# Top-k attention and routed experts on one core: where the pieces of one search stand among those of the next

## The chip, the cores and the metric

The kernel runs on one core of a Trainium2 chip. The metric is the device time of one execution in microseconds (us). Three executions of the kernel before took 1707.5, 1709.06 and 1711.37 us; the median is 1709.06.

PE is the matrix engine, DVE the vector engine, ACT the scalar engine, POOL GpSimd, SP the engine whose queue issues most of the loads. Each engine takes its instructions in order and stands at the first whose input or buffer is not there.

## The reference

Attention over 8 batches, 8 heads, 576 tokens, 64 wide, in which each row keeps only its 32 largest scores; then a layer of 8 experts, one per token.

```python
def _attn_ref(q, k, v):
    scores = scale * np.matmul(q, k.transpose(0, 1, 3, 2))
    kth = np.partition(scores, -top_k, axis=-1)[..., -top_k:-top_k + 1]
    scores = np.where(scores >= kth, scores, -1000000000.0)
    attn = np.exp(scores - np.max(scores, axis=-1, keepdims=True))
    attn = attn / (np.sum(attn, axis=-1, keepdims=True) + 1e-09)
    return np.matmul(attn, v)

def _moe_ref(x, w_gate, w1, w2):        # x: 4608 tokens x 512
    logits = x @ w_gate
    expert_idx = np.argmax(logits, axis=1)
    ...
    for e in range(E):                  # tokens sorted by expert
        h = np.maximum(x_sorted[lo:hi] @ w1[e], 0.0)
        y_sorted[lo:hi] = h @ w2[e]
    return gate_w[:, None] * y_sorted[inv_perm]
```

## The kernel before

The work of attention is cut into 32 units, one for a batch and two heads. The 576 rows of a head are four tiles of 128 and a rest of 64. A unit has five searches: four over a pair of tiles (the same tile of both heads) and one over the single tile that holds both rests. So there are 160 searches, five to a unit and twenty to a batch.

One search goes through all engines. PE multiplies scores (`products`, L234). ACT copies them from PSUM (`scores`, L243, tile `s`). DVE folds each row into halves, the larger and the smaller of two elements (`fold`, L250 and L251, tile `hl`), and finds the 32nd largest in four rounds of `max` and `match_replace` (`search`, L273 to L295, result `thr`). POOL makes `low` from it (L297). ACT turns scores below the threshold into a huge penalty (`depths`, L309, tile `w`), POOL subtracts (`less`, L318) and ACT takes the exponential (`weights`, L329). PE transposes the weights (`transposed`: the four large blocks `wTm`, L342, then the rest `wTl`, L350), and ACT copies both back (L345, L347, L353, L355).

After its last search a unit has an end (`outputs`, `ending`): the products with `v` in two halves of the query columns (`po`, L372), the copy to `oT` (L375), transposes and gate logits (`px`, `pl`, copied to `lt` and `x`), the divisors on DVE (L397 to L400), the logits and the scaled rows on POOL (`logits`, L405 to L408, and `rows`, L416). The last unit of a batch also routes it (`route`): DVE takes the largest logit (`mx`, L421) and ranks the tokens, and five indirect DMAs from POOL scatter the rows into `x_rows`, sorted by expert (L466).

An expert block is 128 rows of one expert: a load of rows and weights (`load_block`, on SP's queue), 16 pieces on PE (eight of `ph`, L572, and eight of `py`, L581), the result `y` on ACT (L584) and a store by an indirect DMA from POOL (L585). Batches from the third on have blocks of rows already sorted: 4, 4, 5, 4, 5 and 4 of them are computed a few pieces at a time between the searches (`pieces`), 14 after them, the last two of the former being kept back for the routing of the last batch.

The order on PE, ACT and DVE is the order of the code in `loop` (`tc.manual_schedule`). Scores are multiplied four searches ahead and copied three ahead. In search `i` come the DVE part, `depths` and `less` of `i`, the transposes of `i - 1`, half of the expert pieces, the copies of the scores of `i + 3` between the exponentials of `i`, the products of `i + 4`, and the other half of the pieces. The steps of a unit's end are a generator that goes on at named places (`at_place`). On POOL only the instructions marked `in_turn` keep the program's order; a store is put behind the last subtraction known, and a planner places it.

Of the kernel before, what the change touches and what calls it, by code (L numbers as in the profile page):

```python
# [9 lines left out]
F32 = mybir.dt.float32  # L10
# [33 lines left out]
def kernel(  # L44
# [98 lines left out]
    def token_ids(t, b):  # L143
        nc.gpsimd.iota(t, pattern=[[P, KC]], base=b * S, channel_multiplier=1)
# [30 lines left out]
    scattered = []  # L175
# [158 lines left out]
    def transposed(n, tiles, w):  # L334
        pair = len(tiles) == 2
# [3 lines left out]
        for m, i in enumerate(tiles):  # L339
# [17 lines left out]
    def outputs(n, x):  # L357
# [3 lines left out]
        po = []  # L361
        for j in range(2):
            q = slice(j * HF, (j + 1) * HF)
            po.append(bank("po"))
            for c in range(KC):
                for h in range(2):
# [5 lines left out]
                    nc.tensor.matmul(po[j][r, 0:HF], lhsT, rhs, start=(c == 0), stop=(c == KC - 1))  # L372
# [45 lines left out]
    def route(x, lg):  # L418
# [45 lines left out]
        def scatter(i):  # L464
# [5 lines left out]
            if not k.exact:  # L470
                tc.add_manual_dep(put, k.last_pool.name, AFTER)
                for other in mine:
                    tc.declare_no_dep(put, other, reason="the rows of one batch go to different places")
                mine.append(put)
# [63 lines left out]
    def load_block(expert, piece):  # L538
# [5 lines left out]
        if not k.exact:  # L544
            for put in scattered:
                tc.add_manual_dep(got, put.name, WAIT)
        n.w1 = k.wp.tile([P, 1, DT, F], F32, name="w1")
# [13 lines left out]
    def block(n, following=lambda: None):  # L561
# [23 lines left out]
        put = nc.gpsimd.indirect_dma_start(  # L585
            out=out[:, :], out_offset=bass.IndirectOffsetOnAxis(ap=n.x[:, 0, Dm + 1:XW].bitcast(I32), axis=0),
            in_=y[:, :], in_offset=None, bounds_check=N - 1, oob_is_err=False,
        )
        if not k.exact:
            tc.add_manual_dep(put.ins, k.last_pool.name, AFTER)  # L590

    PIECES = 2 * FT
    FIRST = 10
    ARRIVED = 10
# [3 lines left out]
    with ExitStack() as st:  # L598
# [9 lines left out]
        waiting, loaded, coming, spare, scatters = [], [], [], [], []  # L608
        current = None
# [5 lines left out]

        def following():
            if loaded:
                turned(loaded[0])

        def pieces(n):  # L620
            nonlocal current, left
            while n > 0 and left > 0:
                if current is None:
# [3 lines left out]
                    current = block(now, following)  # L627
                    ahead()
                if next(current, "end") == "end":
# [15 lines left out]
        def ending(b, u):  # L645

            n = unit[b * U + u]
            if u == 0:
                x_of[b] = k.xp.tile([P, KC, XW], F32, name="x")
                token_ids(x_of[b][:, :, Dm + 1].bitcast(I32), b)  # L650
# [244 lines left out]
```

## Time and profile before

| | |
|---|---|
| median of three runs | 1709.06 us |
| profiled execution | 1716.52 us, span 1714.6 us |
| PE, DVE, ACT, POOL busy | 1429.6, 1306.2, 928.1, 672.6 us |
| weight loads on PE busy | 916.1 us |
| mean granted clock of PE | 0.887 |
| DMA, all queues | 230.65 MB, mean 135 GB/s |

The span is the time from the first to the last instruction. Busy time is a share of the whole span, in which the attention part (the first 1,420 us) and the expert part (the rest) have different limits. An instruction's idle time is that of its engine just before it; behind the arrow stands what ended it. A line such as L318 is a line of the kernel above.

### The profile page before, as it was taken

What the parts mean: (1) busy time and instruction counts of PE and PEld (TensorE: products, weight loads), DVE (VectorE), ACT (ScalarE), POOL (GpSimd) and SP (SyncE); (2) the same over time, 40 slices, a digit from 0 to 9 for tenths busy, and PEclk for the clock granted to TensorE, in tenths of its full rate; (3) what the DMA queues carried; (4) which work ended last, traced back from release to release, by engine and by line L of the source; (5) the groups of instructions that cost most, each with busy time, mean ns of one, the idle gap of its engine ahead of it and who ended that gap; (6) DMA issues with size and microseconds to landing.
All of it is one profiled execution on the core that took longest, in us unless ns stands there. A gap on an engine that the chain in (4) does not pass through costs nothing. (4 is left out here: it accounts for less than half of the span.)

```text
span 1714.6 us, 24871 instructions
## 1 busy us (share of the span) xinstructions
PE 1429.6 (83%) x7874; PEld 916.1 (53%) x7874; DVE 1306.2 (76%) x4261; ACT 928.1 (54%) x1937; POOL 672.6 (39%) x993
## 2 busy tenths in 40 slices
PE   5788777867898899879987899889888889699996
PEld 3444444434555555545555555556555556477664
DVE  7999999989998899889968999889869992000000
ACT  4666666656676576656655676556655663111111
POOL 2444454435444545444434545444434453000000
PEclk8666677666999899989998999899999999899998
DMA  1000010004333433324433334343542424788884
GB/s 57 23 22 22 28 44 22 23 28 137 138 132 139 149 138 133 139 98 165 156 132 137 135 133 143 134 148 139 186 167 69 139 108 180 273 297 310 314 297 148
DMA packets 102188, 230.65 MB, mean 135 GB/s; under 512 B 5150, under 2 KB 25630, under 8 KB 102048
## 3 DMA queue, kind: packets, MB, share of 16 engines
q1 hardware_dynamic: 95904, 210.06, 34.4%
q0 software_dynamic: 6144, 18.92, 3.0%
q8 instruction: 64, 1.05, 0.3%
q14 instruction: 76, 0.62, 0.1%
HBM read 207.68 MB, written 22.33 MB: 134 GB/s over the span
## 5 line engine op out<-in xcount | busy, mean ns | idle before, releaser
L318 POOL TENSOR_TENSOR w<-s,w 128x576 f32<-128x576 f32 x288 | 412.2, 1450 | 264.9 <-ACT w L309 264.1
L234 PE MATMUL sc<-qkb 64*128 64x288 f32 (+1 forms) x1280 | 344.4, 514 | 70.9 <-ACT s L243 61.7
L273 DVE MAX8 tops<-scr 128x8 f32<-128x288 f32 x864 | 355.4, 448 | 2.2
L581 PE MATMUL py<-w,hT 128*128 128x512 f32 x640 | 319.3, 629 | 8.9 <-ACT hT L577 8.7
L572 PE MATMUL ph<-xTs,w 128*128 128x128 f32 x2560 | 312.2, 280 | 1.4 <-DMA w<-in_moe_w_dram 0.7
L572 PEld LDWEIGHTS ph<-xTs,w 128*128 128x128 f32 x2560 | 302.5, 196 | 16.4 <-issue 15.4
L309 ACT ACTIVATE w<-s,low 128x576 f32<-128x576 f32 x288 | 209.3, 770 | 180.7 <-POOL low L297 179.7
L234 PEld LDWEIGHTS sc<-qkb 64*128 64x128 f32 (+1 forms) x1280 | 172.3, 210 | 223.5 <-ACT s L243 173.6
L282 DVE MATCH_REPLACE8 scr<-tops,scr 128x288 f32<-128x288 f32 x576 | 251.0, 443 | 0.0
L329 ACT ACTIVATE w<-w,nbias 128x576 f32<-128x576 f32 x288 | 224.4, 780 | 0.3 <-POOL w L318 0.3
L342 PEld LDWEIGHTS wTm<-ident,w 128*128 128x128 f32 x1152 | 150.5, 159 | 85.6 <-issue 67.0
L342 PE MATMUL wTm<-ident,w 128*128 128x128 f32 x1152 | 187.2, 309 | 10.5 <-ACT x L391 7.3
L345 ACT COPY wT<-wTm 128x512 f32<-128x512 f32 x256 | 139.2, 583 | 92.5 <-PE wTm L342 92.4
L243 ACT COPY s<-sc 128x576 f32<-128x576 f32 x288 | 181.4, 631 | 9.8 <-PE sc L234 9.8
L581 PEld LDWEIGHTS py<-w,hT 128*128 128x128 f32 x640 | 115.2, 197 | 126.7 <-issue 111.3
L585 POOL DMA_INDIRECT out_dram<-y,xg x40 | 46.0, 1150 | 345.5 <-ACT y L584 323.3
L372 PE MATMUL po<-wT,vb 128*64 128x288 f32 x1024 | 156.3, 453 | 24.2 <-ACT wT L347 24.2
L250 DVE TENSOR_TENSOR hl<-s 128x576 f32<-128x576 f32 (+1 forms) x160 | 134.0, 837 | 40.6 <-ACT s L243 40.6
L350 PE MATMUL wTl<-ident,w 128*64 128x128 f32 x288 | 70.7, 323 | 111.8 <-ACT wT L345 111.6
L297 POOL TENSOR_SCALAR low<-thr 128x2 f32<-128x2 f32 (+1 forms) x160 | 36.5, 228 | 254.8 <-DVE thr L295 219.4
L282 DVE MATCH_REPLACE8 scr<-tops,hl 128x288 f32<-128x288 f32 x288 | 125.4, 442 | 0.0
L372 PEld LDWEIGHTS po<-wT,vb 128*64 128x64 f32 x1024 | 74.3, 150 | 95.6 <-ACT wT L347 35.2
(123 smaller groups left out, 1359.8 us busy)
## 6 DMA issues: line engine op xcount, KB each, us to landing
w<-in_moe_w_dram SPq DMA_DIRECT2D x80, 2048.0 KB, 12.4
qkb<-in_qk_dram SPq DMA_DIRECT2D x32, 576.0 KB, 3.7
xg<-x_rows SPq DMA_DIRECT2D x40, 257.0 KB, 2.8
vb<-in_v_dram SPq DMA_DIRECT2D x32, 320.0 KB, 3.1
x_rows<-blank SPq DMA_DIRECT2D x9, 257.0 KB, 2.9
x_rows<-x,posi POOLq DMA_INDIRECT x40, 3.1
out_dram<-y,xg POOLq DMA_INDIRECT x40, 3.0
wg<-in_moe_w_gate_dram SPq DMA_DIRECT2D x1, 16.0 KB, 1.9
```

Of the source, the lines that this page charges most:

```text
L234: nc.tensor.matmul(ps[rows, j, 0:HF], n.q[d, cols], n.k[d, j * HF:(j + 1) * HF], start=True, stop=True)
L243: lambda m=m, ps=ps: nc.scalar.copy(s[:, m, :, :], ps[:, :, 0:HF]) for m, ps in enumerate(got)
L273: nc.vector.max(out=tops[:, m, r * 8:(r + 1) * 8], in_=src[m])
L282: nc.vector.match_replace(out=scr[:, m, :], in_to_replace=tops[:, m, r * 8:(r + 1) * 8], in_values=src[m], imm_value=NEG,)
L309: nc.scalar.activation(w[:, m, :], s[:, m, :, :].rearrange("p j k -> p (j k)"), AF.Relu, scale=-STEEP, bias=low[:, m:m + 1],)
L318: k.last_pool = in_turn(nc.gpsimd.tensor_tensor(w[:, m, :], s[:, m, :, :].rearrange("p j k -> p (j k)"), w[:, m, :], op=ALU.subtract)).ins
L329: nc.scalar.activation(w[:, m, :], w[:, m, :], AF.Exp, scale=scale, bias=nbias[:, m:m + 1], accum_out=n.z[:, c + m:c + m + 1],)
L342: nc.tensor.transpose(pm[:, c * P:(c + 1) * P], w[:, m, c * P:(c + 1) * P], ident)
L345: nc.scalar.copy(n.wT[:, :, m, tiles[0] * P:(tiles[0] + 1) * P], pm4)
L372: nc.tensor.matmul(po[j][r, 0:HF], lhsT, rhs, start=(c == 0), stop=(c == KC - 1))
L572: nc.tensor.matmul(ph[:, f, :], n.w1[:, 0, dt, fc * P:(fc + 1) * P], n.xT[:, dt, :], start=(dt == 0), stop=(dt == DT - 1),)
L581: nc.tensor.matmul(py, hT[:, f, :], n.w2[:, 0, f, :], start=(f == 0), stop=(f == FT - 1))
```

## The change

A unit's end now begins after its fourth pair, not after the single tile. The first half of the output products needs only the queries of the first three pairs and is issued there; each half is copied to `oT` right behind `depths`, at a new place `"relu"`. The second half follows after the single tile's transposes. The divisors come one search later and POOL's logits one search later than before, and so does the routing; `FIRST` and `ARRIVED`, the searches at which a batch's new blocks begin, go from 10 to 12.

The copies of scores stand right behind `depths` and ahead of the copies of the transposes. The expert pieces of a search are spread anew over the five searches of a unit (`share`), also over the one that had none, and their first half stands between `wTm` and `wTl`. The fold of the single tile and that of the next unit's first pair both stand in the search of the fourth pair; the single tile has a buffer of its own (`hl1`).

A block's `y` is made at the start of the next pieces or behind the next subtraction, and its store is put off to the next call of `put_stores`, behind a subtraction or in the middle of the next block. Token numbers keep the program's order on POOL. Scatters no longer wait for loads of blocks that were fetched before.

```diff
@@ fold
-        hl = k.att.tile([P, 2, 2, HF], F32, name="hl")
+        hl = k.att.tile([P, 2, 2, HF], F32, name="hl") if len(tiles) == 2 else k.att.tile([P, 2, 1, HF], F32, name="hl1", bufs=1)
@@ transposed, between the copies of wTm and the transposes wTl
+        yield
@@ outputs
         for j in range(2):
             q = slice(j * HF, (j + 1) * HF)
-            po.append(bank("po"))
+            po = bank("po")
...
             yield
-        for j in range(2):
-            nc.scalar.copy(oT[:, j * HF:(j + 1) * HF], po[j][:, 0:HF])
+            nc.scalar.copy(oT[:, q], po[:, 0:HF])
             yield
@@ block
-            yield
+            yield "last" if f == FT - 1 else None
...
+        put_off(store)
+        def put_stores():
+            nonlocal current, ended
+            while stores:
+                stores.pop(0)()
+            if ended == "last":
+                ended = next(current, "end")
+                current = None
@@ ending
+            yield "products"
             next(out_steps)
+            yield "relu"
+            next(out_steps)
+            yield "weights"
             yield "products"
             next(out_steps)
...
             yield "weights"
             next(out_steps, None)
+            yield "small"
+            divisors(n)
             yield "begun"
             logits(n, lg)
             rows(n, x)
@@ loop
                 def between():
-                    if i + 1 < len(work):
-                        hl_of[i + 1] = fold(work[i + 1][2], s_of[i + 1])
+                    if len(g) == 2:
+                        fold_to(i + 1 if i + 1 < len(work) and len(work[i + 1][2]) == 2 else i + 2)
...
                 less(g, s_of.pop(i), w_of[i])
+                put_stores()
                 scatter(1)
+                at_place("relu")
...
+                share = 0.5 if g in (groups[0], groups[-2]) else 1.6 if g == groups[2] else 1.2 if g == groups[1] else 1
+                now = max(0, min(int(credit * share + 0.5), room))
+                credit = min(credit - now, 4 * rate)
+                if i + AHEAD < len(work):
+                    s_of[i + AHEAD], steps = scores(got_of.pop(i + AHEAD))
+                    for step in steps:
+                        step()
                 at_place("turn")
                 if i:
-                    turn(i - 1)
...
-                weights(n, g, w_of[i], nbias, steps)
+                    turns = turning(i - 1)
+                    next(turns)
+                pieces(now - now // 2)
+                if i:
+                    next(turns, None)
+                weights(n, g, w_of[i], nbias)
                 if i + AHEAD + 1 < len(work):
                     multiply(i + AHEAD + 1)
+                if g == groups[-2]:
+                    end = ending(b, u)
+                    late.append([end, next(end)])
                 at_place("products")
                 at_place("weights")
-                pieces(now - now // 2)
+                pieces(now // 2)
```

On POOL, around the first store of an expert block; before, it stands behind the subtraction of the second search after a unit, and the logits (`lt`, `lg`, `x`) of that unit right behind it.

```order
L275 TENSOR_SCALAR nbias<-tops_88 128x2
L297 TENSOR_SCALAR low<-thr 128x2
L300 TENSOR_TENSOR over<-tops_88,thr 128x2
L318 TENSOR_TENSOR w<-s,w 128x576 x2
L585 DMA out_dram<-y,xg 4608x512
L275 TENSOR_SCALAR nbias<-tops_90 128x2
L405 TENSOR_TENSOR lt<-lt,rz_98 128x80
L407 TENSOR_TENSOR lg<-lg,lt 128x40
L408 TENSOR_TENSOR lg<-lg,lt 128x40
L416 TENSOR_TENSOR x<-x,rz_98 128x5x128
L297 TENSOR_SCALAR low<-thr 128x2
```

Now, at the same place:

```order
L275 TENSOR_SCALAR nbias<-tops_90 128x2
L297 TENSOR_SCALAR low<-thr 128x2
L300 TENSOR_TENSOR over<-tops_90,thr 128x2
L318 TENSOR_TENSOR w<-s,w 128x576 x2
L590 DMA out_dram<-y,xg 4608x512
L275 TENSOR_SCALAR nbias<-tops_92 128x2
L405 TENSOR_TENSOR lt<-lt,rz_98 128x80
L407 TENSOR_TENSOR lg<-lg,lt 128x40
L408 TENSOR_TENSOR lg<-lg,lt 128x40
L416 TENSOR_TENSOR x<-x,rz_98 128x5x128
L297 TENSOR_SCALAR low<-thr 128x2
```

The rows are alike, but the search they belong to is one later: `tops_92` where it was `tops_90`.

On PE, from a pair's transposes to the end of a unit, in the part where expert pieces (`ph`, `py`) run beside the searches; before:

```order
L342 MATMUL wTm<-ident,w 128x128 x8
L350 MATMUL wTl<-ident,w 64x128 x2
L581 MATMUL py<-w_5311,hT 128x512
L234 MATMUL sc<-qkb 128x288 x4
L581 MATMUL py<-w_5311,hT 128x512
L342 MATMUL wTm<-ident,w 128x128 x4
L350 MATMUL wTl<-ident,w 64x128
L372 MATMUL po<-wT,vb 64x288 x8
L372 MATMUL po<-wTt,vb 64x288 x2
L234 MATMUL sc<-qkb 64x288 x4
L372 MATMUL po<-wT,vb 64x288 x8
L372 MATMUL po<-wTt,vb 64x288 x2
```

And now:

```order
L373 MATMUL po<-wT,vb 64x288 x8
L373 MATMUL po<-wTt,vb 64x288 x2
L343 MATMUL wTm<-ident,w 128x128 x8
L575 MATMUL ph<-xTs,w_5365 128x128 x8
L352 MATMUL wTl<-ident,w 64x128 x2
L234 MATMUL sc<-qkb 128x288 x4
L560 MATMUL xtp<-ident,xg 128x128 x4
L584 MATMUL py<-w_5367,hT 128x512
L343 MATMUL wTm<-ident,w 128x128 x4
L584 MATMUL py<-w_5367,hT 128x512
L352 MATMUL wTl<-ident,w 64x128
L234 MATMUL sc<-qkb 64x288 x4
```

The first half of the output products stands ahead of the transposes of the unit's last pair, the second half follows these rows, and pieces of an expert block (two of `ph`, one of `py`) stand between `wTm` and `wTl`.

On DVE, inside the short search of the first unit's single tile, after its third `match_replace`; before:

```order
L273 MAX tops_92<-scr 128x8
L282 MATCH_REPLACE scr<-tops_92,scr 128x288
L250 TENSOR_TENSOR hl<-s 128x576
L251 TENSOR_TENSOR hl<-s 128x576
L273 MAX tops_92<-scr 128x8
```

And now, in the search of the pair before it:

```order
L282 MATCH_REPLACE scr<-tops_90,scr 128x288 x2
L250 TENSOR_TENSOR hl_1064<-s 128x288
L251 TENSOR_TENSOR hl_1064<-s 128x288
L250 TENSOR_TENSOR hl<-s 128x576
L251 TENSOR_TENSOR hl<-s 128x576
L273 MAX tops_90<-scr 128x8 x2
```

The next unit's first pair (128x576) is folded right behind the single tile (128x288).

## Rows read from the trace of the kernel before

**Rows 1.** The page: busy time of the engines, and DVE in 40 slices.

```profile
PE 1429.6 (83%) x7874; PEld 916.1 (53%) x7874; DVE 1306.2 (76%) x4261; ACT 928.1 (54%) x1937; POOL 672.6 (39%) x993
...
DVE  7999999989998899889968999889869992000000
```

**Rows 2.** Waits of DVE, 64 to 1423 us: total us, times, longest.

```profile
DVE mx L421 <- POOL lg L408: 41.1, 7, 13.4
DVE hl L250 <- ACT s L243: 34.8, 20, 4.5
```

**Rows 3.** Stretches: length, busy of PE, PEld, DVE, ACT, POOL, clock, DMA, GB/s.

```profile
64.00:438.00 374.00, 286.93 (x1276) 160.91 (x1274) 360.16 (x1169) 235.34 (x499) 172.59 (x261) 0.69 0.15 50
438.00:614.80 176.80, 151.71 (x896) 96.72 (x893) 163.76 (x535) 112.88 (x237) 82.58 (x120) 0.95 0.32 115
614.80:793.60 178.80, 153.06 (x903) 96.98 (x900) 164.62 (x534) 113.08 (x239) 84.25 (x121) 0.95 0.38 134
793.60:984.70 191.10, 164.33 (x970) 109.19 (x966) 163.47 (x535) 112.85 (x239) 82.91 (x121) 0.95 0.42 150
984.70:1164.30 179.60, 154.86 (x922) 98.16 (x919) 166.35 (x534) 115.61 (x243) 85.12 (x123) 0.95 0.37 133
1164.30:1355.60 191.30, 163.19 (x974) 108.13 (x969) 163.43 (x535) 112.81 (x240) 83.24 (x120) 0.96 0.42 150
1355.60:1422.90 67.30, 57.85 (x383) 41.68 (x379) 60.78 (x192) 44.65 (x96) 35.24 (x53) 0.95 0.39 137
1422.90:1479.90 57.00, 39.38 (x242) 27.15 (x241) 8.81 (x50) 12.54 (x29) 10.36 (x13) 0.91 0.49 169
1479.90:1714.60 234.70, 214.56 (x1192) 152.87 (x1192) 0.00 (x0) 34.72 (x57) 14.68 (x15) 0.97 0.76 277
```

**Rows 4.** Stretches of one unit, without and with expert blocks.

```profile
227.60:267.60 40.00, 30.39 (x141) 16.99 (x140) 39.16 (x124) 26.06 (x56) 20.37 (x30) 0.75 0.10 33
614.80:655.40 40.60, 37.06 (x234) 23.62 (x229) 39.32 (x125) 28.44 (x62) 19.94 (x29) 1.00 0.39 140
```

**Rows 5.** Instructions in order of time, 900 to 904 us: start, length.

```profile
901.02 1.04 POOL L585 DMA_INDIRECT out_dram<-y,xg  x1 [13.56 <-ACT y L584]
...
903.34 0.20 DVE L421 TENSOR_REDUCE mx<-lg 128x5 f32<-128x40 f32 x1 [13.44 <-POOL lg L408]
```

**Rows 6.** Waits of POOL, 64 to 1423 us.

```profile
POOL out_dram L585 <- ACT y L584: 78.2, 16, 13.6
```

**Rows 7.** Waits of PE, 64 to 1423 us.

```profile
PE wTl L350 <- ACT wT L345: 105.1, 103, 6.4
PE sc L234 <- ACT s L243: 54.2, 80, 1.2
```

**Rows 8.** Instructions in order of time, from the last threshold to the tail.

```profile
1417.84 0.16 DVE L295 TENSOR_REDUCE thr<-both 128x1 f32<-128x9 f32 x1
...
1432.11 0.60 PE L342 MATMUL wTm<-ident,w 128*128 128x128 f32 x4
...
1479.91 1.08 PE L557 MATMUL xtp<-ident,xg 128*128 128x128 f32 x4 [15.35 <-DMA xg<-x_rows]
```

**Rows 9.** The page's costliest groups: busy us, mean ns, idle before.

```profile
L243 ACT COPY s<-sc 128x576 f32<-128x576 f32 x288 | 181.4, 631 | 9.8 <-PE sc L234 9.8
...
L372 PE MATMUL po<-wT,vb 128*64 128x288 f32 x1024 | 156.3, 453 | 24.2 <-ACT wT L347 24.2
```

**Rows 10.** Instructions in order of time, 643.5 to 646 us.

```profile
643.54 1.40 POOL L318 TENSOR_TENSOR w<-s,w 128x576 f32<-128x576 f32 x1 [3.67 <-ACT w L309]
643.64 1.92 DVE L250 TENSOR_TENSOR hl<-s 128x576 f32<-128x576 f32 x1
...
645.48 0.75 DVE L251 TENSOR_TENSOR hl<-s 128x576 f32<-128x576 f32 x1
```

**Rows 11.** Groups by shape on DVE, 64 to 1423 us.

```profile
L250 DVE TENSOR_TENSOR hl<-s 128x576 f32<-128x576 f32 x121 | 105.2, 869 | 34.8 <-ACT s L243 34.8
...
L250 DVE TENSOR_TENSOR hl<-s 128x288 f32<-128x288 f32 x31 | 22.4, 723 | 0.0
```

More of the change, by code (lines that the diff above doesn't have):

```diff
@@ L143, in token_ids @@
     def token_ids(t, b):
-        nc.gpsimd.iota(t, pattern=[[P, KC]], base=b * S, channel_multiplier=1)
+        return nc.gpsimd.iota(t, pattern=[[P, KC]], base=b * S, channel_multiplier=1)
     NTOP = 4
@@ L473, in scatter @@
                     tc.declare_no_dep(put, other, reason="the rows of one batch go to different places")
+                for other in fetched:
+                    tc.declare_no_dep(put, other, reason="new rows go behind all full blocks")
                 mine.append(put)
@@ L559, in turned, with block @@
         nc.scalar.copy(n.xT, ps)
-    def block(n, following=lambda: None):
+    def block(n, following=lambda: None, put_off=lambda store: store()):
         if not hasattr(n, "xT"):
@@ L607 @@
         x_of, lg_of = {}, {}
-        waiting, loaded, coming, spare, scatters = [], [], [], [], []
-        current = None
+        waiting, loaded, coming, spare, scatters, stores = [], [], [], [], [], []
+        current = ended = None
         left = 0
@@ L620, in pieces @@
         def pieces(n):
-            nonlocal current, left
+            nonlocal current, left, ended
+            if ended == "last":
+                ended = next(current, "end")
+                current = None
             while n > 0 and left > 0:
@@ L626, in pieces @@
                         turned(now)
-                    current = block(now, following)
+                    current = block(now, following, stores.append)
                     ahead()
-                if next(current, "end") == "end":
+                ended = next(current, "end")
+                if ended == "end":
                     current = None
@@ L658, in ending @@
                 load_values(unit[b * U + u + 2])
-            yield "weights"
-            next(out_steps)
-            yield "small"
-            divisors(n)
-            yield "turn"
+            yield "relu"
             next(out_steps)
@@ L695, in ending, with turning @@
                 scatter(0)
-        late, place = None, None
+        late = []
         def at_place(name):
-            nonlocal place
-            if place == name:
-                place = next(late, None)
+            for end in list(late):
+                if end[1] == name:
+                    end[1] = next(end[0], None)
+                    if end[1] is None:
+                        late.remove(end)
         got_of, s_of, hl_of, w_of = {}, {}, {}, {}
-        def turn(i):
+        folded = set()
+        def turning(i):
             b, u, g = work[i]
-            transposed(unit[b * U + u], g, w_of.pop(i))
+            return transposed(unit[b * U + u], g, w_of.pop(i))
         def multiply(i):
@@ L714, in multiply, with fold_to @@
                 unit.append(load_unit(*units[b * U + u + 2]))
+        def fold_to(i):
+            for j in range(i + 1):
+                if j < len(work) and j not in folded:
+                    folded.add(j)
+                    hl_of[j] = fold(work[j][2], s_of[j])
         def loop():
-            nonlocal late, place, credit, rate
+            nonlocal credit, rate
             for i in range(min(AHEAD, len(work))):
@@ L723, in loop @@
             multiply(AHEAD)
-            hl_of[0] = fold(work[0][2], s_of[0])
+            fold_to(0)
             for i, (b, u, g) in enumerate(work):
@@ L782 @@
         pieces(ALWAYS * PIECES)
-        for _ in current:
-            pass
+        put_stores()
+        put_stores()
         any_p = k.small.tile([P, 1], F32, name="any_p")
@@ L832 @@
                         weights(n, g, w, nbias)
-                        transposed(n, g, w)
+                        for _ in transposed(n, g, w):
+                            pass
                     for _ in outputs(n, x):
```

51 lines of the change are left out of this document (22 added, 29 removed).

## The prediction

> **What bounds the kernel now.** I read the engine table and the slices first, then DVE's waits, then a table of stretches, and only then single places. The engine table says little by itself: PE is the busier engine over the whole, DVE the second [rows 1]. The slices split the program in two: DVE is at nine tenths or close to it from the second slice to the thirty-third and does nothing in the last six, where only expert blocks are left on PE [rows 1]. So the first 1,420 us are the top-32 search on DVE, and the last 235 us are PE alone. What the change can shorten is the first part, and the passage between the two.
>
> DVE's waits between 64 and 1,423 us have two causes: the routing of a batch waits for POOL's logits, 41.1 us in seven waits, and a fold waits for the copied scores, 34.8 us in 20 [rows 2]. I cut the span where DVE starts `doubt` (L397), which happens once per unit of work (five searches), so that a stretch is a whole number of units, and call a stretch without expert blocks bare, one with four blocks per batch light, one with five heavy [rows 3]. The bare stretch of nine units is 374.0 us with 360.2 busy on DVE. The three light stretches of four units are 176.8, 178.8 and 179.6. The two heavy ones are 191.1 and 191.3, though DVE has no more to do there (163.5 and 163.4 busy, against 163.8 to 166.4). PE does have more, 164 against 152 to 155.
>
> A unit that nothing disturbs shows what is left when the waits go: 0.84 us idle on DVE in 40.0 bare, 1.28 in 40.6 light, and there PE is idle 3.54 [rows 4]. Everything above these is what the change may win.
>
> Where the waits come from is seen at 901 us. POOL stood 13.56 us at the store of an expert block's output, since ACT had not yet made `y`; the logits were queued behind the store, and DVE stood 13.44 us for them [rows 5]. POOL waited so 78.2 us in all in this part [rows 6]. Whatever POOL holds back (`low`, the subtraction) comes late to ACT and then to PE: PE waited 105.1 us for ACT's copy before the small transposes `wTl` and 54.2 for the copied scores [rows 7].
>
> **The change part by part.**
>
> Stores in fixed places, `y` earlier, logits one search later. The store now stands behind the subtraction of a search, at least one search after the block ended, and the logits go to POOL two searches after their copy from PSUM instead of one. The store itself still costs POOL its 1.04 us [rows 5], beside idle time. What is queued behind it is `nbias` and, in one search of each unit, the logits; `low`, which ACT waits for, follows them but is due some 8 us later, a fifth of a unit of 40. This removes the POOL wait, and with it most of both DVE waits. Token numbers and the undeclared order between scatter and block loads only take away waits of POOL; I cost them at nothing.
>
> Bare stretch: 374.0 less 360.2 leaves 13.8 idle; nine units at 0.84 keep 7.6. Gain **6**.
>
> Light stretches: 535.2 in all, DVE busy 494.7, idle 40.5; twelve units at 1.28 keep 15.4. Gain **25**. Bounds: 10 if more than half of the waits come back in other shapes, 40 if the remaining idle goes too.
>
> Heavy stretches: 382.4 in all. DVE's floor is 326.9 and eight units at 1.28, so 337. PE's floor is its busy time, 327.5, and what it must idle. PE takes over here, so its idle time decides. Between nothing and the 3.54 of an undisturbed light unit I take 2 per unit, because expert pieces now stand between the large transposes `wTm` and `wTl`, so that ACT's copy has a cover of one to four pieces where it had none. That gives 343.5. Gain **39**; bounds 27 (at 3.54) and 45 (DVE's floor).
>
> Last stretch (67.3, DVE idle 6.5): the first pieces of a batch now come two searches later, so six more pieces fall into these 1.6 units. A piece is worth 0.7 of PE, from the heavy stretches' mean of 163.8 against the first two light ones' 152.4, over 16 pieces more. 4.2 more on PE's 57.9, with 2 idle per unit, makes 65. Gain **2**.
>
> Passage to the tail (57.0 us): the chain goes from the last threshold at 1417.84 through the last transposes at 1432.11 to the first tail block at 1479.91, and PE idles 15.35 at its end [rows 8], so what is cut from the chain comes off the time as far as that idle time lasts. Half of a unit's output products move ahead of the last search: 156.3 us over 32 units is 4.9, so 2.4 for a half [rows 9]. A store no longer stands before the logits, 1.0. The 14.3 us from threshold to transposes are mostly backlog: the one subtraction in them needs 1.4 [rows 10]. I take a third off, 4.6. Gain **8**, bounds 0 and 16 (nothing, or all but those 1.4).
>
> Folds. A pair's fold is 0.75 us alone and was 1.92 beside POOL's subtraction [rows 10]; the mean over 121 is 869 ns and of the half-width ones 723 [rows 11]. Over 0.75 and half of that, the first fold instruction of each search loses 121 x 0.12 + 31 x 0.35 = 25 us. The pair that was folded inside the short search of a single tile now goes one search earlier, behind that tile's own fold, so the short search meets the subtraction no more. I take half of the loss, less the heavy stretches where PE decides: gain **11**. Bounds: 25 gained, or 25 more lost, if the four folds in a row meet POOL's work of their own search.
>
> Splitting the copies of scores from the exponentials adds and removes no instruction; its cost is the order on ACT alone, and is in the PE idle time above and in a rival below. Output halves free a PSUM bank earlier; nothing waits for it in the rows, so nothing is counted.
>
> The sum is 6 + 25 + 39 + 2 + 8 + 11 = 91 us. The profiled execution took 1716.5 us (span 1714.6), so 1625.5 for it. The median of the three runs shown is 1709.1, 7.5 lower; a median is what will be compared, so I forecast **1618**.
>
> **Rivals.**
>
> PE becomes the engine for good. For it: PE is 85% busy in the light and heavy stretches, and its work is now cut into more, smaller pieces. Against it: the undisturbed light unit has 3.54 us to spare. If the heavy stretches gain nothing and the light ones half, 91 - 39 - 12 = 40: 1669.
>
> The folds collide more. POOL's logits and row scaling move to the very search that now has four folds in a row (2.25 us by 0.75 and its half). If one fold per unit is held as at 643.64 us, 1.17 us times 31 is 36, and the 11 are not gained: 1618 + 47 = 1665. Against it: the row scaling stood beside a fold before, too. The rule for this is in the Trainium skill, page "SBUF — State Buffer", section "Who interferes with whom": a VectorE instruction with two inputs in SBUF and a GpSimd one that reads SBUF exclude each other for a whole instruction, whichever came first. By that rule, the trace agrees: the subtraction had begun 0.10 us before the fold that took 1.92.
>
> Slower: the scores' copies now stand before ACT's copies of the transposes. Each search of a pair puts two of them at 631 ns [rows 9], 1.26 us, between `wTm` and `wTl`. The light, heavy and last stretches hold 21.6 units and so 86 such searches: 109 us on PE. Its idle time of 3.54 per unit takes 76; 33 are left, DVE's waits return as waits for scores, and only the bare stretch and the passage gain 14: 1709 + 33 - 14 = 1728. It decides from the point at which fewer than two pieces (1.4 us) stand between the two transposes. The new order has one to four there, and the one only beside the single tile, where PE has the output products besides. So it is unlikely.
>
> Better: the unit falls to DVE's floor everywhere, 6 + 40 + 45 + 2 + 14 + 20 = 127: 1582.
>
> **How the numbers follow.** The forecast and what lies near it, 57%; PE as the engine, 17%; better, 13%; colliding folds, 7%; slower, 4%; the waits merely change places and nothing comes of it, 2%. The forecast's own range is 1600 to 1640. With the better case partly in and the two near 1665 almost, I give 1596 to 1660. Differences of up to 0.2% cannot be told from none for this kernel. Faster 95%, same 1%, slower 4%.
>
> **What would show it.** Right: POOL's wait for `y` before the tail under 15 us; DVE's wait for logits under 8; PE's wait for the copy before `wTl` halved; the four units of a light stretch near 168 us and of a heavy one near 172; the last threshold to the first tail block under 52. Wrong: heavy stretches over 182 (PE is the engine), or the folds' mean over 0.95 us, or new waits of PE at `wTl` of over 1 us per search.

## The result, and the profile after

Four executions of the changed kernel took 1629.21 us in the median (1624.39 to 1631.53), beside 1710.21 us (1707.5 to 1712.86) for the kernel before: a ratio of 0.9523 [0.9495, 0.955], 81 us faster. The profiled execution took 1630.09 us (span 1628.1, mean granted clock 0.896), 86.4 us less than the one of before.

The page of the changed kernel, engines and DVE's slices, answers to [rows 1]:

```profile
PE 1334.4 (82%) x7874; PEld 869.4 (53%) x7874; DVE 1285.3 (79%) x4261; ACT 916.7 (56%) x1937; POOL 672.9 (41%) x993
...
DVE  7999999999999999999998999999989972000000
```

DVE has the same 4261 instructions and 20.9 us less busy time. They fill the same 34 slices, but a slice is now 40.7 us long instead of 42.9. PE has the same 7874 and 95 us less busy time, which no step of the prediction counted on.

Stretches of the changed kernel, with the columns and the rule for the cuts of [rows 3] (`doubt` now stands one search later, so the first cut is 7.3 us later too):

```profile
71.30:430.60 359.30, 237.06 (x1263) 137.38 (x1263) 347.85 (x1169) 230.62 (x499) 174.47 (x261) 0.75 0.15 49
430.60:598.70 168.10, 146.43 (x904) 96.64 (x904) 162.71 (x535) 111.70 (x238) 84.19 (x120) 0.92 0.36 128
598.70:769.80 171.10, 150.08 (x902) 96.06 (x902) 164.04 (x535) 112.11 (x238) 83.80 (x121) 0.91 0.39 140
769.80:940.70 170.90, 152.34 (x976) 101.31 (x976) 162.27 (x535) 113.01 (x241) 83.74 (x122) 0.96 0.47 168
940.70:1110.50 169.80, 148.09 (x913) 95.78 (x911) 162.89 (x535) 112.47 (x240) 82.16 (x121) 0.94 0.40 141
1110.50:1281.80 171.30, 152.89 (x975) 101.79 (x975) 162.67 (x534) 112.95 (x241) 83.81 (x122) 0.95 0.46 164
1281.80:1338.20 56.40, 50.94 (x325) 35.58 (x324) 51.95 (x167) 37.11 (x79) 30.07 (x46) 0.97 0.37 139
```

A heavy stretch now takes as long as a light one, 168 to 171 us: DVE, busy for 162 to 164 of them, sets both. DVE's waits in 71.3 to 1338.2 us, beside [rows 2]:

```profile
DVE base L445 <- ACT rk L440: 7.3, 7, 2.2
DVE hl L250 <- ACT s L243: 6.5, 2, 3.2
```

The waits for the logits are gone and those for the scores fell from 34.8 us to 6.5. The longest in total are now the routing's waits for ACT's copy of the ranks (`rk`), which were 1.1 us before. POOL's list of waits for the same stretch has no wait for `y` (78.2 before, [rows 6]). But PE waits as long as it did [rows 7]:

```profile
PE wTl L352 <- ACT wT L346: 110.3, 48, 6.1
```

It waits seldom and long instead of often and briefly, and DVE no longer has to wait with it.

### The profile page after: what moved, and what is told of

It is laid out like the page before. It is cut to its first block, busy times and chain, and to the rows that moved or that the text cites. A ratio compares the mean times of both kernels' runs of the same rounds, so it can differ in the third digit from the quotient of the medians.

```text
span 1628.1 us, 25051 instructions
## 1 busy us (share of the span) xinstructions
PE 1334.4 (82%) x7874; PEld 869.4 (53%) x7874; DVE 1285.3 (79%) x4261; ACT 916.7 (56%) x1937; POOL 672.9 (41%) x993
## 5 line engine op out<-in xcount | busy, mean ns | idle before, releaser
L318 POOL TENSOR_TENSOR w<-s,w 128x576 f32<-128x576 f32 x288 | 405.2, 1426 | 289.4 <-ACT w L309 289.4
L575 PEld LDWEIGHTS ph<-xTs,w 128*128 128x128 f32 x2560 | 300.1, 193 | 26.8 <-issue 25.1
L584 PE MATMUL py<-w,hT 128*128 128x512 f32 x640 | 308.7, 614 | 5.5 <-ACT hT L580 5.4
L234 PE MATMUL sc<-qkb 64*128 64x288 f32 (+1 forms) x1280 | 244.1, 506 | 69.4 <-ACT s L243 63.1
L343 PE MATMUL wTm<-ident,w 128*128 128x128 f32 x1152 | 179.6, 295 | 43.2 <-ACT oT L375 34.1
L234 PEld LDWEIGHTS sc<-qkb 64*128 64x128 f32 (+1 forms) x1280 | 124.0, 208 | 142.8 <-ACT s L243 80.2
L343 PEld LDWEIGHTS wTm<-ident,w 128*128 128x128 f32 x1152 | 138.7, 150 | 110.7 <-ACT oT L375 40.7
L297 POOL TENSOR_SCALAR low<-thr 128x2 f32<-128x2 f32 (+1 forms) x160 | 34.8, 217 | 353.2 <-DVE thr L295 329.2
L243 ACT COPY s<-sc 128x576 f32<-128x576 f32 x288 | 169.9, 637 | 9.6 <-PE sc L234 9.6
L373 PE MATMUL po<-wT,vb 128*64 128x288 f32 x1024 | 171.7, 488 | 0.6 <-ACT wT L348 0.6
L352 PE MATMUL wTl<-ident,w 128*64 128x128 f32 x288 | 65.3, 303 | 124.9 <-ACT wT L346 123.7
L250 DVE TENSOR_TENSOR hl<-s 128x576 f32<-128x576 f32 (+1 forms) x160 | 129.7, 811 | 12.0 <-ACT s L243 12.0
L373 PEld LDWEIGHTS po<-wT,vb 128*64 128x64 f32 x1024 | 80.9, 164 | 88.7 <-issue 34.1
```

The costliest lines, as they stand in the source:

```text
L234: nc.tensor.matmul(ps[rows, j, 0:HF], n.q[d, cols], n.k[d, j * HF:(j + 1) * HF], start=True, stop=True)
L243: lambda m=m, ps=ps: nc.scalar.copy(s[:, m, :, :], ps[:, :, 0:HF]) for m, ps in enumerate(got)
L318: k.last_pool = in_turn(nc.gpsimd.tensor_tensor(w[:, m, :], s[:, m, :, :].rearrange("p j k -> p (j k)"), w[:, m, :], op=ALU.subtract)).ins
L343: nc.tensor.transpose(pm[:, c * P:(c + 1) * P], w[:, m, c * P:(c + 1) * P], ident)
L373: nc.tensor.matmul(po[r, 0:HF], lhsT, rhs, start=(c == 0), stop=(c == KC - 1))
L575: nc.tensor.matmul(ph[:, f, :], n.w1[:, 0, dt, fc * P:(fc + 1) * P], n.xT[:, dt, :], start=(dt == 0), stop=(dt == DT - 1),)
```

## The experiments

All ratios are to the kernel before on the same chip. Losses are differences of these ratios times 1714 us, the time of before beside these runs; the changed kernel's own ratio is uncertain by 0.003, or 5 us, and so is each loss measured against it. Waits are read from 64 to 1330 us; in slower runs the attention part lasts longer, so there this window leaves out more of it.

| run | what is different from the changed kernel | median us | ratio |
|---|---|---|---|
| e1_store_at_once | `y` and store at the block's end | 1642.5 | 0.9576 [0.9563, 0.9589] |
| e4_logits_early | divisors, logits, routing a search earlier | 1633.59 | 0.9513 [0.9495, 0.9531] |
| e9_store_and_logits_back | both | 1676.87 | 0.9788 [0.9764, 0.9811] |
| e2_copies_between | score copies between the exponentials | 1791.69 | 1.0468 [1.0447, 1.0489] |
| e6_pieces_after | no pieces between `wTm` and `wTl` | 1657.99 | 0.9671 [0.9653, 0.9689] |
| e8_copies_and_pieces_back | both | 1689.58 | 0.9863 [0.9841, 0.9885] |
| e10_four_back | all four | 1743.77 | 1.0158 [1.0132, 1.0184] |
| e5_before_stores_off | the kernel before, with late stores alone | 1697.0 | 0.9908 [0.9892, 0.9925] |
| e3_folds_apart | folds where they were | 1631.4 | 0.9514 [0.9499, 0.9529] |
| f1_even_shares | pieces spread more evenly | 1624.37 | 0.9498 [0.9484, 0.9512] |
| f2_cover_fourth | f1, more pieces in one gap | 1627.32 | 0.9504 [0.9482, 0.9527] |
| f3_cover_and_early_logits | f2 with e4 | 1630.99 | 0.953 [0.9517, 0.9543] |

**The stores and the logits.** First each undone alone.

```diff
-                    current = block(now, following, stores.append)
+                    current = block(now, following)
...
-                if ended == "end":
+                if ended == "last":
+                    next(current, "end")
+                    ...
```

> The changed kernel, but y and its store are issued at once when an expert block's last piece is done, as before the change; all else stays. Theory A (the store that waits for y holds up POOL, and most of DVE's waits come from there): POOL waits 50 us or more for y again before the tail, DVE waits 30 to 60 us more, about 1665 us. Theory B (the waits went because the logits have one search more, and the copies of the scores stand earlier): POOL waits for y, but DVE does not feel it, 1630 to 1638 us.

It lost 9 us. POOL waits for `y` again, but DVE's waits hardly change: it stands 11.3 us for scores and not at all for logits. The loss is in DVE's busy time. From the first `doubt` to the last this run takes 18 us longer (the passage behind wins 8 back, see below), and there the same 4000 instructions of DVE were busy 1233.5 us instead of 1214.4; the single tile's second fold instruction (L251) rose from 606 to 993 ns, the pairs' `both` (L291) from 227 to 316. That these meet POOL's work, which the store has shifted, is likely and was not shown. POOL's wait in this run, 64 to 1330 us:

```profile
POOL out_dram L590 <- ACT y L587: 58.2, 9, 9.0
```

```diff
             yield "weights"
+            yield "small"
+            divisors(n)
             yield "relu"
...
-            yield "small"
-            divisors(n)
             yield "begun"
```

> The changed kernel, but the divisors, POOL's logits and the routing come one search earlier, where they were before. Theory A (stores were the cause of the routing's wait): DVE waits for logits at most 10 us in all, 1625 to 1640 us. Theory B (the extra search is what hides the logits): DVE waits 3 to 6 us in each of seven routings again, 1650 to 1670 us.

It cost nothing (the intervals overlap): 13.3 us of waiting for logits came back on DVE, but the wait for scores fell to 2.0 and the one for the ranks is gone.

Then both undone, and the late store alone on the kernel before.

```diff
-                    current = block(now, following, stores.append)
+                    current = block(now, following)
...
             yield "weights"
+            yield "small"
+            divisors(n)
...
```

> The changed kernel with two parts undone that cost 10 and 1 us when undone alone: y and its store at once, and divisors, logits and routing one search earlier. Theory A (each covers for the other: with the store in front and no extra search the routing waits again): DVE waits 20 to 40 us for logits before the tail, 1655 to 1680 us. Theory B (the two are independent): the sum of both, 1640 to 1650 us.

Together they cost 45 us, where the parts cost 9 and nothing. DVE's and POOL's waits of this run, 64 to 1330 us:

```profile
DVE hl L250 <- ACT s L243: 35.7, 12, 6.1
DVE mx L421 <- POOL lg L408: 20.4, 7, 5.0
...
POOL out_dram L590 <- ACT y L587: 90.0, 12, 10.7
```

A store without data only holds up what stands behind it. With the logits a search later there is slack behind it; with the store a search later there is nothing to be held up. Either cover hides most of the wait, so undoing one shows little of what the two are worth.

The change of `block`, `pieces` and `put_stores`, put into the kernel before:

```diff
-        put = nc.gpsimd.indirect_dma_start(
+        def store():
+            put = nc.gpsimd.indirect_dma_start(
...
+        put_off(store)
@@ loop, behind less
+                put_stores()
```

> The kernel before, with one part of the change: y is made and its store put off as in the changed kernel. Theory A (the store that waits for y is the root of the waits of the kernel before): POOL's wait for y before the tail goes from 78 to under 15 us, DVE's 76 us of waits to under 35, 1660 to 1680 us. Theory B (the order of copies and pieces on ACT and PE is the root, and the store one of several covers): the routing's 41 us shrink to 15 to 25, the folds' waits stay, 1685 to 1705 us.

It gained 16 us, ratio 0.9908. POOL's wait for `y` is gone from this run's list; DVE's waits, 64 to 1330 us, 41.1 us for logits and 32.9 for scores before, are only thinned:

```profile
DVE mx L421 <- POOL lg L408: 29.9, 7, 7.9
DVE hl L250 <- ACT s L243: 29.7, 14, 5.0
```

So the store was a cause of the 13 us waits [rows 5], and not the root of most of DVE's waiting.

**The copies of scores and the pieces.**

```diff
-                if i + AHEAD < len(work):
-                    s_of[i + AHEAD], steps = scores(got_of.pop(i + AHEAD))
-                    for step in steps:
-                        step()
                 at_place("turn")
...
-                weights(n, g, w_of[i], nbias)
+                steps = []
+                if i + AHEAD < len(work):
+                    s_of[i + AHEAD], steps = scores(got_of.pop(i + AHEAD))
+                weights(n, g, w_of[i], nbias, steps)
```

> The changed kernel, but the copies of the scores go back between the exponentials. Theory A (the copies' place matters little as long as expert pieces cover the transposes): PE's wait for scores grows, DVE's units stay, 1625 to 1636 us. Theory B (the early copies are what lets PE run on): PE idles 1 us more per search, heavy stretches grow by 8 us each, 1645 to 1660 us.

It lost 162 us and is slower than the kernel before. Its waits on DVE, PE and ACT, 64 to 1330 us:

```profile
DVE hl L250 <- ACT s L243: 104.9, 22, 11.3
...
PE sc L234 <- ACT s L243: 179.5, 199, 7.9
...
ACT wTt L355 <- PE wTl L352: 88.3, 80, 3.3
```

One search of this run in order of time shows the ring that closes:

```profile
658.20 1.95 PE L575 MATMUL ph<-xTs,w 128*128 128x128 f32 x16
...
659.99 0.38 PE L352 MATMUL wTl<-ident,w 128*64 128x128 f32 x2
...
660.40 0.36 ACT L355 COPY wTt<-wTl 64x256 f32<-64x256 f32 x1 [1.42 <-PE wTl L352]
...
660.67 0.63 ACT L243 COPY s<-sc 128x576 f32<-128x576 f32 x1
...
661.36 0.75 PE L234 MATMUL sc<-qkb 64*128 64x288 f32 x2 [0.99 <-ACT s L243]
...
662.65 1.23 PE L234 MATMUL sc<-qkb 64*128 64x288 f32 x6 [0.54 <-ACT s L243]
```

The expert pieces (`ph`) put off `wTl`; ACT stands at its copy `wTt`, and the copies of scores stand behind that one; PE then has no PSUM bank for the next scores and stands in turn. In the changed kernel the same place reads:

```profile
602.97 1.16 ACT L243 COPY s<-sc 128x576 f32<-128x576 f32 x2
...
604.67 0.41 PE L352 MATMUL wTl<-ident,w 128*64 128x128 f32 x2
...
605.01 1.24 PE L234 MATMUL sc<-qkb 64*128 64x288 f32 x8
```

The score copies are done before ACT can be caught at `wTt`, and the eight products run in one go, busy 1.24 us instead of 0.75 + 1.23. ACT waits at `wTt` in the changed kernel too, 75.3 us in 77 waits beside 88.3 in 80; what differs is what is queued behind that wait, and PE's waits for the copies of scores are 57.6 us there beside 179.5. Without the pieces between (e8, below) ACT's wait is 2.8 us.

```diff
                     next(turns)
-                pieces(now - now // 2)
-                if i:
                     next(turns, None)
+                pieces(now - now // 2)
```

> The changed kernel, but the first half of the expert pieces stands behind both transposes, not between them. Theory A (the pieces between are the cover that keeps PE running): PE waits 60 us or more longer for ACT's copy before the small transposes, heavy stretches over 180 us, 1645 to 1665 us. Theory B (with the copies of the scores early, the order of pieces matters little): heavy stretches 170 to 176 us, 1624 to 1638 us.

It lost 25 us: PE's waits before `wTl` are back, 115 of them where the changed kernel has 49 in this window (110.6 us). On DVE the waits for scores rose from 6.5 us to 20.4, those for the ranks from 7.3 to 12.8, and the mean of the pairs' first fold instruction from 822 ns to 922. PE's waits of this run, 64 to 1330 us:

```profile
PE wTl L352 <- ACT wT L346: 157.1, 115, 6.1
```

```diff
-                    for step in steps:
-                        step()
...
-                pieces(now - now // 2)
-                if i:
                     next(turns, None)
+                pieces(now - now // 2)
...
+                weights(n, g, w_of[i], nbias, steps)
```

> The changed kernel with both undone: copies of the scores between the exponentials, and pieces behind both transposes. Theory A (the loss with late copies comes from the two together: pieces delay the small transposes, ACT stands at their copy, the copies of the scores stand behind it, and PE then stands at the scores): most of that loss goes, 1635 to 1670 us, PE's wait for scores under 100 us. Theory B (late copies alone cost it): 1760 us or more.

Both undone lose 58 us, far less than the copies undone alone: pieces between the transposes are worth 25 us with early copies and cost 104 with late ones (1.0468 less 0.9863). The early copies pay by themselves: e6, which has them without the pieces between, is 33 us faster than this run. The pieces between pay only with them.

**What is left without the four.** Here the edits of e8 and e9 are undone together; the output halves, the shares, the late ends and the folds stay.

```diff
-                    current = block(now, following, stores.append)
+                    current = block(now, following)
...
-                    for step in steps:
-                        step()
...
+                weights(n, g, w_of[i], nbias, steps)
...
```

> The changed kernel with four parts undone together: copies of the scores between the exponentials, pieces behind both transposes, y and store at once, and logits and routing one search earlier. What stays is the output halves, the fold of single tile and pair together, the shares, and the token numbers. Theory A (these four parts are the whole gain, and what stays is worth nothing): within 1% of the kernel before, 1700 to 1725 us. Theory B (what stays is worth 20 us or more of its own): 1690 us or less. If the losses of the two pairs, 57 and 44 us, simply add: 1734 us.

It is 27 us slower than the kernel before. The losses of the two pairs, 58 and 45, add up to 103; measured are 109 (each uncertain by some 5 us). So the pairs are nearly independent, and without them the rest of the change does not pay. Which of its parts costs the 27 us was not taken apart.

**The folds.**

```diff
                 def between():
-                    if len(g) == 2:
-                        fold_to(i + 1 if i + 1 < len(work) and len(work[i + 1][2]) == 2 else i + 2)
+                    fold_to(i + 1)
```

> The changed kernel, but each search folds for the next one only, so the pair after a single tile is folded inside the single tile's short search, as before. Theory A (that fold meets POOL's subtraction; the bare stretch lost 10 us of such excess): 1640 to 1650 us, the excess of fold instructions up by 10 to 20 us. Theory B (the excess went because the subtraction runs earlier): no change, 1625 to 1634 us.

The time is the same. The folds did get dearer, and nothing came of it. First the changed kernel's, then this run's, 71.3 to 1338.2 us:

```profile
L250 DVE TENSOR_TENSOR hl<-s 128x576 f32<-128x576 f32 x120 | 98.7, 822 | 6.5 <-ACT s L243 6.5
```

```profile
L250 DVE TENSOR_TENSOR hl<-s 128x576 f32<-128x576 f32 x120 | 103.6, 863 | 0.0
```

Moving the fold saves 4.9 us on L250 and 4.0 on L251, and leaves the single tile's as it is (791 and 795 ns). The changed kernel, which folds faster, waits 6.5 us for scores and 7.3 for the ranks; this run waits 10.5 us for the logits and 0.8 for the ranks.

**Two attempts to go on.** In the light stretch from 598.7 us PE stands idle in the fourth search and then runs at half its clock (last section). f1 spreads the pieces evenly over the searches, so that more stand there, and issues the stores that are left ahead of the last transposes; f2 puts all pieces of that search between the transposes; f3 adds the earlier logits. The code shown for f2 and f3 leaves out what they share with f1.

```diff
-                share = 0.5 if g in (groups[0], groups[-2]) else 1.6 if g == groups[2] else 1.2 if g == groups[1] else 1
+                share = 0.5 if g == groups[0] else 1.2 if g == groups[1] else 1.1
...
+            put_stores()
+            put_stores()
             for _ in turning(len(work) - 1):
```

> The changed kernel with the expert pieces spread more evenly (weights 0.5, 1.2, 1.1, 1.1, 1.1 over the five searches instead of 0.5, 1.2, 1.6, 0.5, 1), so that two pieces instead of one stand between the transposes in a unit's fourth search of a light stretch, and with the last y and store before the last transposes. Theory A (in light stretches PE idles 2.8 us there, its clock then drops to half for 6.8 us, the second half of the output products comes late, and the subtraction meets the next fold): the clock in light stretches rises from about 0.92 to over 0.96, the excess of folds falls by 4 us per light stretch, and the tail starts 5 us earlier, 1612 to 1622 us. Theory B (the drop of the clock is harmless, and the folds meet the subtraction for another reason): only the tail's 5 us, 1622 to 1628 us.

```diff
-                pieces(now - now // 2)
+                first = now if g == groups[-2] else now - now // 2
+                pieces(first)
...
-                pieces(now // 2)
+                pieces(now - first)
```

> As the run with evener shares, and in the fourth search all pieces (three or four) stand between the transposes. Theory A (the idle time there is what drops the clock): no stretch of half clock is left in most units of the light stretches, light stretches at 163 to 166 us, 1608 to 1618 us. Theory B: the pieces moved there delay the first half of the output products instead, and nothing is gained over the evener shares.

```diff
+                first = now if g == groups[-2] else now - now // 2
...
+            yield "small"
+            divisors(n)
             yield "relu"
```

> As the run before, and divisors, logits and routing one search earlier, which alone cost nothing but had less collision of folds in the light stretches (4 to 7 us of excess where the changed kernel has 8 to 11). Theory A (POOL's logits and row scaling collide with the four folds of the fourth search, and moving them away helps): 4 to 8 us below the run before. Theory B (the routing's wait that returns, 13 us, eats it): the same or up to 5 us above.

f1 has the lowest median of all, 1624.37 us, but its interval meets the changed kernel's, so a gain of 4 us is likely and not shown. f2 and f3 bring nothing beyond it.

## Why the prediction was right, and where it was wrong

The direction and the size were right, and the range held the time. Of the 11 us between the forecast of 1618 and the 1629.2 measured, 4.6 are the sum (91 forecast, 86.4 between the two profiled executions), and the rest is the step from profile to median: the profiled execution of before lay 7.5 us above the median shown, and I took that off the forecast as if it were constant, while that of the changed kernel lies 0.9 above its own. That the sum came so close is in part luck: by the stretches above, the bare one gave 9 us more than forecast, the folds' 11 us did not come, and the passage with the expert part after it gave 6 less than forecast.

**Light stretches: right, 25 forecast, 26.2 measured.** They take 509.0 us against 535.2. DVE's idle time fell from 40.5 to 19.4 (15.4 forecast), and its busy time gave the other 5: not the folds, which rose from 96.3 us to 102.1; its largest fall is in `both` (L291), from 23.1 to 16.7. The cause was too narrow, though. I took the store for the source of most waits; e5 puts the store alone at 16 us over the whole program; with the slack behind it, it is worth 45 (e9), and the copies with the pieces are worth 58 (e8).

**Heavy stretches: right in size, 39 forecast, 40.2 measured, by a wrong step.** I took PE's busy time of 327.5 us for PE's floor and added two idle microseconds per unit. Measured are 342.2 us in all with PE busy for 305.2 and idle for 37, 4.6 per unit. The floor was none: busy time of PE fell where its matmuls came to stand together. The scores in the first heavy stretch, in the kernel before and then in the changed one:

```profile
L234 PE MATMUL sc<-qkb 64*128 64x288 f32 x128 | 27.2, 453 | 1.9 <-ACT s L243 1.6
```

```profile
L234 PE MATMUL sc<-qkb 64*128 64x288 f32 x128 | 19.9, 429 | 0.0
```

The same 128 instructions are busy 7.3 us less, 27%, while the mean of one fell by only 5%; the rest is that they overlap more. The Trainium skill, page "Perfetto Trace Analysis", section "Identifying the Most-Contended Engine", warns against this number as a measure of how close PE is to its peak, and goes by the useful arithmetic and the weight loads' busy share instead. The trace agrees: by the latter share PE had room in this stretch, 109.19 us of 191.10 before [rows 3] and 101.31 of 170.90 now. What sets these stretches now is DVE, busy for 324.9 of the 342.2.

**Bare stretch: 6 forecast, 14.7 measured, by another cause.** Its idle time fell by only 2.4 us (13.8 to 11.4); its busy time fell by 12.3, and that is the folds: the pairs' took 60.8 us before and 54.4 now, the single tiles' 15.8 and 9.8. The pairs' folds, in the kernel before, in the changed one and in e2_copies_between:

```profile
L250 DVE TENSOR_TENSOR hl<-s 128x576 f32<-128x576 f32 x36 | 31.4, 873 | 0.0
L251 DVE TENSOR_TENSOR hl<-s 128x576 f32<-128x576 f32 x36 | 29.4, 817 | 0.0
```

```profile
L251 DVE TENSOR_TENSOR hl<-s 128x576 f32<-128x576 f32 x36 | 27.2, 757 | 0.0
L250 DVE TENSOR_TENSOR hl<-s 128x576 f32<-128x576 f32 x36 | 27.2, 756 | 0.0
```

```profile
L251 DVE TENSOR_TENSOR hl<-s 128x576 f32<-128x576 f32 x36 | 34.0, 944 | 0.0
L250 DVE TENSOR_TENSOR hl<-s 128x576 f32<-128x576 f32 x36 | 29.6, 821 | 0.5 <-ACT s L243 0.5
```

With the score copies early the pairs' folds run at their undisturbed 0.75 us; with the copies late they do not (63.6 us in e2, 61.5 in e8), and the stretch, cut at `doubt` as above, takes 372.3 us in e2 and 371.7 in e8, against 361.7 with only the folds put back (e3). So the order of the copies on ACT, which I had costed at nothing of its own, is worth some 10 to 13 us here, where no expert piece runs; beside the changed kernel, DVE is busy 7 to 8 us longer in e2 and e8 and idle 5 us longer. Why the later copies lengthen the folds was read from no row and stays open. The single tiles' folds stay short with late copies (9.9 us in e2, 9.0 in e8), so their 6 us have another cause; 2.6 of them are lost again with the logits a search earlier (e4), and the rest stays open.

**Folds: 11 forecast, nothing measured.** This is the term that was wrong. The first fold instruction of a pair got shorter, 869 to 822 ns [rows 11], but the second got longer, 790 to 827, and all folds from the first `doubt` to the last took 240.7 us before and 241.3 now. What the bare stretch won, 12.4 us, was lost where expert blocks run: 96.3 to 102.1 in the light stretches, 57.0 to 65.1 in the heavy ones. The move of the fold by itself (e3) changes no time. The term did not follow from its own rows either: half of 25 us, less the heavy stretches' eight of 31 units, is 9. Where expert blocks run the collisions stayed. An example of the changed kernel:

```profile
626.27 3.31 POOL L318 TENSOR_TENSOR w<-s,w 128x576 f32<-128x576 f32 x2 [4.18 <-ACT w L309]
626.98 1.32 DVE L250 TENSOR_TENSOR hl<-s 128x576 f32<-128x576 f32 x1
628.23 1.96 DVE L251 TENSOR_TENSOR hl<-s 128x576 f32<-128x576 f32 x1
```

Both folds of this search meet the subtraction and take 3.2 us instead of 1.5. The Trainium skill, page "SBUF — State Buffer", section "Who interferes with whom", has two such instructions exclude each other; this trace agrees. The rival built on it (1665 us) did not come: the single tiles' folds rose from 39.9 us to 43.3 in all.

**Passage and last stretch.** The last stretch is 10.9 us shorter, of which 7.3 are the later cut: 3.6, where 2 were forecast. From the last threshold to the first tail block the chain of [rows 8] fell from 62.1 us to 57.0; under 52 was the mark, so the forecast of 8 was missed. (Its largest part, 4.6 for "a third" of 14.3 us, should have been 4.8, or 4.3 without the 1.4 that must stay; that changes nothing.) These rows of the changed kernel are its ends and its middle:

```profile
1335.05 0.16 DVE L295 TENSOR_REDUCE thr<-both 128x1 f32<-128x9 f32 x1
...
1354.37 0.27 POOL L408 TENSOR_TENSOR lg<-lg,lt 128x40 f32<-128x40 f32 x1
...
1359.41 0.77 DVE L445 TENSOR_TENSOR base<-base,rk 128x8 f32<-128x8 f32 x4 [2.36 <-ACT rk L440]
...
1367.96 0.91 POOL L466 DMA_INDIRECT x_rows<-x,posi  x1 [0.30 <-issue]
...
1377.41 8.18 SPq L487 DMA_DIRECT2D x_rows<-blank  x8
...
1392.01 1.09 PE L560 MATMUL xtp<-ident,xg 128*128 128x128 f32 x4 [15.29 <-DMA xg<-x_rows]
```

And in the kernel before the three in the middle:

```profile
1444.61 0.27 POOL L408 TENSOR_TENSOR lg<-lg,lt 128x40 f32<-128x40 f32 x1
...
1456.25 0.90 POOL L466 DMA_INDIRECT x_rows<-x,posi  x1 [0.30 <-issue]
...
1464.18 8.79 SPq L485 DMA_DIRECT2D x_rows<-blank  x8
```

Threshold to logits fell from 26.8 us to 19.3, nearly the 8 forecast. From the logits to the last scatter it rose from 11.6 to 13.6, mostly because DVE waits 2.36 us for ACT's copy of the ranks, where it waited 0.74, and from there to the fill-up from 7.9 to 9.5. In e1 the same chain took 48.9 us, 8 less, so that run won back in the passage part of what it lost before; why was not taken apart. The expert part after it is 1.4 us longer (236.1 beside 234.7).

**The rivals.** PE as the engine did not come, as the heavy stretches show. The slower rival had the sign of its own step reversed: it charged the early copies with 109 us on PE, and it is the late copies that delay PE (e2). Its condition, few pieces between the transposes, does cost, 25 us (e6), and stays far from a loss. The forecast that PE's wait before `wTl` would be halved was wrong: 105.1 us became 110.3. Most of it lies in the bare stretch, where there are no pieces to stand between. PE's waits where expert blocks run, 440 to 1330 us, in the changed kernel:

```profile
PE sc L234 <- ACT s L243: 36.7, 5, 8.2
PE wTl L352 <- ACT wT L346: 35.8, 15, 3.5
```

There the wait before `wTl` fell from 59.4 us to 35.8, but the one for scores rose from 18.8 to 36.7, in five long waits. Neither bounds the unit, since DVE has its folds' input in time.

## What to carry to other kernels

On an engine that works in order, put the copies that free a producer's buffers ahead of those that wait for that same producer, before anything is put between the producer's steps: here the pieces without the early copies cost 104 us, the early copies without the pieces gained 33, and together they gained 58. When an edit is tried alone and seems worth little, undo it together with the edit that gives slack at the same place: the late store and the late logits cost 9 us and nothing alone, and 45 together. And do not take the busy time of the second engine for its floor.

## What the runs showed of the hardware

A short idle time of PE was followed by half its clock. In the fourth search of a unit only one piece stood between the transposes; the changed kernel, in order of time:

```profile
612.77 0.64 PE L352 MATMUL wTl<-ident,w 128*64 128x128 f32 x2 [2.77 <-ACT wT L346]
...
613.34 2.29 PE L234 MATMUL sc<-qkb 64*128 64x288 f32 x8
...
615.55 3.79 PE L373 MATMUL po<-wT,vb 128*64 128x288 f32 x16
```

The scores took 2.29 us, where the same eight took 1.24 at 605.01, and ACT then stood 4.02 us for the products `po`. The granted clock of that stretch and of the one behind it (columns as in the stretches above):

```profile
613.00:620.00 7.00, 7.00 (x31) 3.16 (x30) 6.90 (x24) 2.76 (x7) 2.50 (x6) 0.58 1.02 386
620.00:626.00 6.00, 6.00 (x42) 4.46 (x43) 5.86 (x21) 5.15 (x11) 0.38 (x2) 1.00 0.26 101
```

0.58 is close to the lower level, 1.2 GHz, and 1.00 is 2.4 GHz. The fall lies inside the idle time: the granted clock was 1.00 from 610 to 612 us and 0.50 from 612.4. The DMA engines were busy throughout the 7 us too (share 1.02), but they still were from 619 to 620 us, where the clock was 1.00 again. The subtraction at 626.27 then stood beside both folds. That this was a cost worth removing was argued and not shown. In the profiled executions of f1 and f2, which put more pieces there, the light stretch from about 598 us has a clock of 0.95 and 0.96 instead of 0.91, and the three light stretches took 504.9 and 500.8 us instead of 509.0. But over all executions their mean clocks (0.892 to 0.907) meet the changed kernel's (0.896 to 0.903), and by their ratios they are at most 4 us faster.
